# A chain of attention and two MoE layers: dense local attention for the second batch's first 192 rows, sums of squares of weights by TensorE, and rms_g in the split of the normalised x

## The chip, the cores and the metric

One core of one Trainium2 chip runs the whole program. The metric is device time in microseconds of one execution; lower is better. TensorE does the matmuls, VectorE and ScalarE the elementwise steps, GpSimd some products, SyncE (SP) issues every DMA.

## The reference

```python
# attention: q, k, v of (4, 8, 576, 64)
q_d, k_d, v_d = means over 4 rows each            # 144 rows
out_up = repeat(softmax_attention(q_d, k_d, v_d), 4)
scores = scale * q @ k.T, masked to |i - j| < 4
out = out_up + softmax(scores) @ v                # -> x (2304, 512)
# MoE 1: w_in (512, 2048), w_out (2048, 512)
h = x @ w_in; x = (max(h, 0) + alpha * min(h, 0)) @ w_out
# MoE 2: w_gate, w_val (512, 1536), w_out (1536, 512), rms_g (512)
xn = x / sqrt(mean(x * x) + 1e-6) * rms_g
out = (silu(xn @ w_gate) * (xn @ w_val)) @ w_out
```

The kernel takes all inputs as float64 bit patterns (q, k, v as float32) and decodes the weights itself.

## The kernel before, in words

**Tiling.** The 2304 rows are twelve groups of 192 columns, three for each batch; two groups make one of six blocks of 384 columns. `m1` is the first MoE for a block: `h_mm` (L1277) multiplies x by a 128-wide slice of w_in (tile hps), applies the leaky step and splits the result in two fp16 halves (g, ghl), `o_mm` (L1294) multiplies those by w_out (tile acc). `m2` (L1363) is the second MoE: gate and value projections (gps), silu, and the output projection (oacc). Every fp32 operand is split by `split` (L374) into a high and a low fp16 half, one step on ScalarE (L375) and one on VectorE (L376), and a product takes three fp16 matmuls.

**Attention.** Batch 0 goes by the dense path (`Dense`, L702): 96-row windows of scores on TensorE (lsps), exponentials on ScalarE (L889), normalisation, transposes (ltps) and values (lops) on TensorE. Its head tiles T lie in u6 to u9. Groups 3 to 11 go by `local_tasks` (L460): q times seven shifted k on VectorE and GpSimd (L476, six products, alternating), reductions on VectorE (L487), softmax, six products with v (L524), adds on VectorE (L537), transposes on TensorE (L558). The mean-pooled part of batch b is `down(b)`. Group 3, the first 192-column group of batch 1, is staged in the upper slices of wi, since `raw` is not free yet; it is called `l3` and runs beside `down(1)`, ahead of m1.

**Weights.** A `Piece` (L1006) loads a third of a slice in two halves (wr), decodes them (L1048, L1051 on ScalarE, L1053 to L1057 on VectorE) into wc or wo and squares them on ScalarE with an accumulated sum (L1067, tile sqs). The sums over partitions (L349, allps) give a power of two as scale, and the split writes the fp16 halves. w_in has six pieces, w_out six, w_gate, w_val and the second w_out four each. The scale of w_out needs all its squares, so acc matmuls begin after the last. The twelve pieces of the second MoE go through a ring of slots u0 to u12 (`RING`). For gate and value pieces the split multiplies by rms_g as well, one 384-wide quarter at a time (L1188); `rms_tasks` (L1202) normalises x and splits xn (L1259).

**Order.** `m1_first` (L1334) runs the first three h passes of 192 columns (slots h0, h1, h2), then two o passes (o0, o1); the fourth half is `m1(1, CW, CW)` (slot c3). `feed` (L1570) says in which slot background tasks are written. The order in which each engine issues is then set by `issue_order` (L24), a list scheduler with costs per instruction over the whole program; it keeps data dependencies and buffer reuse and reorders everything else. All DMAs stand in SP's one queue. PSUM tiles of tag `at` have two banks.

Of the kernel before, what the change touches and what calls it, by code (L numbers as in the profile page):

```python
# [255 lines left out]
def kernel(  # L256
# [152 lines left out]

    def load_q(g, tag=None):  # L410
        b, t0 = g // CPB, (g % CPB) * T
        t = rawtile([128, 2, T, D], tag, "cq")
        src = bass.AP(tensor=q.tensor, offset=q.offset + b * H * HS + t0 * D,
                      ap=[[TT * D, NC], [2 * HS, HP], [HS, 2], [1, T * D]])
        nc.sync.dma_start(out=t, in_=src)
        return t

    def load_kv(x, g, tag=None):
        b, t0 = g // CPB, (g % CPB) * T
        R = T + 2 * W  # L420
        t = rawtile([128, 2, R, D], tag, "ckv")
        base = x.offset + b * H * HS + (t0 - W) * D

        def part(c0, nc_, h0=0, nh=HP, j0=0, nj=2, nr=R):
            p = HP * c0 + h0
            nc.sync.dma_start(
                out=t[p:p + (nc_ - 1) * HP + nh, j0:j0 + nj, 0:nr],
                in_=bass.AP(tensor=x.tensor, offset=base + c0 * TT * D + (2 * h0 + j0) * HS,
                            ap=[[TT * D, nc_], [2 * HS, nh], [HS, nj], [1, nr * D]]))

        assert b > 0
        if b == B - 1 and t0 + T == TT:
# [27 lines left out]
    def local_tasks(g, engs, tags=(None, None, None), av_pool=True, o_at=None):  # L460
        b, t0 = g // CPB, (g % CPB) * T
# [35 lines left out]
        def sm1():  # L497
            s = st["s"]
            if t0 == 0:
# [3 lines left out]
            if t0 + T == TT:  # L503
# [49 lines left out]
        def trans(half):  # L553
            def f():
# [7 lines left out]
                od = outd_t[b].rearrange("p h (c n) -> p h c n", n=TT // 2)  # L562
                s0 = t0 + half * TH
                for r in range(2):
                    a = s0
                    while a < s0 + TH:
                        o = (r * TT + a) // 4
                        e = a
                        while e < s0 + TH and (r * TT + e) // 4 == o:
                            e += 1  # L570
# [131 lines left out]
    class Dense:  # L702
        def __init__(self, b, place, sd, tsp, smp, lat):
            self.b, self.place, self.sd, self.tsp, self.smp, self.lat = b, place, sd, tsp, smp, lat
            self.st = [{} for _ in range(HP)]

# [143 lines left out]
        def local(self, c, h0, banks):  # L850
# [3 lines left out]
            def s1():  # L854
# [23 lines left out]
                if c:  # L878
                    ls["r"] = raw_p.tile([128, 2 * ns + 2 * CW], F32, tag="raw", name="dls")
                for n, h in enumerate(hs):  # L880
                    tag = ("ob", "xs", "ra", "rb")[h]
                    if c:
# [10 lines left out]
            def s2():  # L893
# [3 lines left out]
                for n, s in enumerate(ls["s"]):  # L897
                    if c:
# [19 lines left out]
            def s4():  # L918
                for n, h in enumerate(hs):
# [8 lines left out]
                    if c:  # L928
# [13 lines left out]
            return [s1, s2, s3, s4]  # L942

# [46 lines left out]
    s1 = const.tile([128, 2 * NF], F32, name="s1")  # L990
    ebw = const.tile([128, NF], F32, name="ebw")
    swi = const.tile([128, NF], F32, name="swi")
    swo = const.tile([128, NF], F32, name="swo")
    s2 = const.tile([128, 3 * NF2], F32, name="s2")
# [8 lines left out]

    sqs = const.tile([128, DM], mybir.dt.bfloat16, name="sqs")

    class Piece:  # L1006
# [53 lines left out]
        def square(self, acc):  # L1060
            for i in range(acc.shape[1]):
                if self.f0 is None:
                    src = self.cv()[:, :, i * 128:(i + 1) * 128]
                    o = sqs.rearrange("p (k c) -> p k c", k=KK)
                else:
                    src, o = self.c[:, i * DM:(i + 1) * DM], sqs
                nc.scalar.activation(out=o, in_=src, func=AF.Square, accum_out=acc[:, i:i + 1])  # L1067
# [3 lines left out]
    RING = (3, 4, 6, 7, 5, 12, 0, 1, 2, 8, 9, 10, 11)  # L1071
# [13 lines left out]
    def prep(p, acc, nsq):  # L1085
# [25 lines left out]
    def scale_out():  # L1111
        x = col(SS + M_WO)
        nc.vector.tensor_reduce(out=x, in_=over_parts(s1[:, NF:2 * NF]), axis=AX.X, op=ALU.add)
# [9 lines left out]
    def split_in(f):  # L1123
# [4 lines left out]
        split(w[:, 0], w[:, 1], c, swi[:, f:f + 1])  # L1128
# [4 lines left out]
    def split_out(f):  # L1133
# [3 lines left out]
        split(w[:, 0], w[:, 1], c, swo[:, f:f + 1])  # L1137
# [7 lines left out]
    gsc = const.tile([128, 8, KK], F32, name="gsc")  # L1145
# [3 lines left out]
    def scale_rg():  # L1149
        nc.vector.tensor_reduce(out=rg2[:, 0:1], in_=rg, axis=AX.X, op=ALU.max, apply_absolute_value=True)  # L1150
        max_parts(rg2[:, 1:2], rg2[:, 0:1])
        nc.vector.tensor_tensor(out=rg2[:, 1:2], in0=rg2[:, 1:2], in1=rg2[:, 1:2], op=ALU.mult)

    def scale2(i):
        def f():
            x = s2[:, 3 * i:3 * i + 3]
            y = s2[:, 3 * i:3 * i + 1]
            nc.vector.tensor_reduce(out=y, in_=over_parts(x), axis=AX.X, op=ALU.max if i < 8 else ALU.add)
            nc.vector.tensor_scalar(out=y, in0=y, scalar1=rg2[:, 1:2] if i < 8 else 1.0, scalar2=LEAST, op0=ALU.mult,
                                    op1=ALU.max)  # L1160
            e, sc_ = eb2[:, i:i + 1], sw2[:, i:i + 1]
            pow2(y, e, sc_, P_W)
            if i < 8:
                nc.vector.tensor_scalar(out=gsc[:, i], in0=rg, scalar1=sc_, scalar2=None, op0=ALU.mult)
                if i < 4:
                    nc.vector.tensor_scalar(out=tsc[:, i:i + 1], in0=e, scalar1=0.5 * 2.0 ** -(P_N + P_W),
                                            scalar2=None, op0=ALU.mult)
            else:
# [3 lines left out]
                nc.vector.tensor_scalar(out=p, in0=p, scalar1=C_INV2, scalar2=None, op0=ALU.mult)  # L1172
# [7 lines left out]
    def split2(i):  # L1180
        def f():
# [3 lines left out]
            if i < 8:  # L1185
# [3 lines left out]
            else:  # L1189
                split(w[:, 0], w[:, 1], p.c, sw2[:, i:i + 1])  # L1190
        return f

    def prep2_tasks():
        out = [[scale_rg]]
        for i in W2_ORDER:
            out.append(prep(p2[i], s2[:, 3 * i:3 * i + 3], 3) + [scale2(i), split2(i)])
# [5 lines left out]
    def rms_tasks(m):  # L1202
# [50 lines left out]
        def xn(e):  # L1253
            def f():
# [4 lines left out]
                split(xh_t[m][:, 0, e], xh_t[m][:, 1, e], x, 2.0 ** P_N)  # L1259
# [103 lines left out]
    def m2(m, slot):  # L1363
# [88 lines left out]
        for tt in range(NT):  # L1452
# [12 lines left out]
            while done < TQ:  # L1465
                b, t = divmod(t_abs + done, TT)
                step = min(TQ - done, TT - t)
                if b == 0:
                    dst = out[b * S + t * NC:b * S + (t + step) * NC, :]
                else:  # L1470
                    dst = bass.AP(tensor=out.tensor, offset=out.offset + (b * S + t) * DM,
                                  ap=[[DM, step], [TT * DM, NC], [1, DM]])
# [36 lines left out]
    def prep_out():  # L1509
        def so(f):  # L1510
# [3 lines left out]
                for t in prep(p, s1[:, NF + 3 * i:min(2 * NF, NF + 3 * i + 3)], min(3, NF - 3 * i))] + [scale_out] + [  # L1514
                    so(f) for f in range(NF)]

    def prep_in(i):
        return prep(p1[i], s1[:, 3 * i:min(NF, 3 * i + 3)], 3 if i < 5 else 1)

    def lane(c):  # L1520
# [3 lines left out]
    pi = [t for p in pi[:3] for t in p] + [lambda: scale_in(0, 9)] + [t for p in pi[3:] for t in p] + [  # L1524
        lambda: scale_in(9, NF)]
# [19 lines left out]
    for h in range(HP):  # L1545
# [5 lines left out]
    wl = wi[:, 8:NF].rearrange("p f a c -> p (f a c)").bitcast(F32)  # L1551
    NQ, NK = 2 * T * D, 2 * (T + 2 * W) * D
    l3 = local(3, tags=(wl[:, 0:NQ], wl[:, NQ:NQ + NK], wl[:, NQ + NK:NQ + 2 * NK]),
               o_at=lambda: p1[5].c[:, KK * 128:KK * 128 + NQ].rearrange("p (t j d) -> p t j d", t=T, j=2))
# [7 lines left out]
    run_all(weave(l3[:-2], d1))  # L1562
    run_all(l3[-2:])
    c1, c2 = lane(1), lane(2)

    def cut(l, at):
# [6 lines left out]
        "h2": po[2] + pr2[0],  # L1573
# [63 lines left out]
```

## Time and profile before

| | before |
|---|---|
| median of 3 runs | 1012.79 us (1012.25 to 1017.23) |
| profiled execution, its own time | 1012.32 us |
| its span | 1010.6 us |
| TensorE, VectorE, ScalarE, GpSimd busy | 930.8, 702.7, 506.8, 147.8 us |

The profiled execution is one run; its span leaves out 1.7 us around the program. PE is TensorE's matmuls, PEld its weight loads, DVE VectorE, ACT ScalarE, POOL GpSimd. A busy TensorE is not TensorE at its peak, as matmuls are pipelined.

### The profile page before, as it was taken

To read this page: it belongs to the slowest core of one execution; us is meant where nothing else is said; L and a number is where in the kernel's file an instruction comes from. 1 tells how busy PE (TensorE), PEld (TensorE's weight loads), DVE (VectorE), ACT (ScalarE), POOL (GpSimd) and SP (SyncE) were. 2 spreads that over 40 slices of the span, in tenths; PEclk is the share of its full clock that TensorE was granted. 3 is DMA by queue.
4 is the path that set the end of the run, shared out by engine and by line. 5 is a ranking of instruction groups with operands and counts; after the bars stand their busy time and mean duration, and the time that the engine had idled before them with its cause. 6 is when DMAs were issued, how large, how long until landed. Compare 5 with 4: busy or idle time off the path is not lost.

```text
span 1010.6 us, 16163 instructions
## 1 busy us (share of the span) xinstructions
PE 930.8 (92%) x6188; PEld 594.4 (59%) x6188; DVE 702.7 (70%) x1482; ACT 506.8 (50%) x1214; POOL 147.8 (15%) x118
## 2 busy tenths in 40 slices
PE   3776777899999999999999999999999999999998
PEld 2554666669976565555656565555556666555454
DVE  3589798999899978999776899983243353442333
ACT  5987879989986473123367232221132432321322
POOL 3522121211001003432100332310000000000000
PEclk9999887899999999999999999999999999999999
DMA  9865228535330143122023111110010000000000
GB/s 257 230 178 186 84 83 276 174 112 157 126 126 13 55 128 104 32 75 67 28 66 96 47 33 47 32 32 1 1 31 1 1 1 1 1 1 4 29 1 31
DMA packets 49821, 74.52 MB, mean 74 GB/s; under 512 B 17532, under 2 KB 30736, under 8 KB 49744
## 3 DMA queue, kind: packets, MB, share of 16 engines
q1 hardware_dynamic: 49744, 73.50, 24.0%
q8 instruction: 48, 0.79, 0.3%
q14 instruction: 29, 0.24, 0.1%
HBM read 68.76 MB, written 4.72 MB: 73 GB/s over the span
## 4 chain that ended last, share of the span: by engine, by line
PE 71%; ACT 11%; DVE 8%; DMA 6%; issue 3%; SPq 1%; POOL 1%; ACTq 0%; POOLq 0%; DVEq 0%
PE gps L1376 22%; PE acc L1297 17%; PE hps L1284 14%; PE oacc L1405 11%; DMA out_dram<-ob 3%; ACT sqs L1067 1%; ACT wr L1048 1%; DVE prod L537 1%; ACT wr L1051 1%; DMA sdv<-in_v_dram 1%; PE lsps L869 1%; SPq L723 1%; ACT dls L889 1%; DMA wr<-in_moe_w_out_dram 1%; PE avps L680 1%
## 5 line engine op out<-in xcount | busy, mean ns | idle before, releaser
L1284 PE MATMUL hps<-xt,wi 128*128 128x192 f16 (+1 forms) x1536 | 336.4, 296 | 9.9 <-DVE g L376 8.2
L1376 PE MATMUL gps<-x,w 128*128 128x384 f16 x1728 | 345.1, 327 | 0.1
L1297 PE MATMUL acc<-ghl,wo 128*128 128x384 f16 (+1 forms) x960 | 251.1, 311 | 4.0 <-ACT ob L1461 2.2
L1376 PEld LDWEIGHTS <-w 128*128 128x128 f16 x1728 | 169.8, 99 | 114.5 <-issue 3.0
L1405 PE MATMUL oacc<-w,uhl 128*128 128x512 f16 x630 | 194.4, 379 | 2.6 <-ACT ob L1461 2.6
L1284 PEld LDWEIGHTS <-wi 128*128 128x128 f16 x1536 | 151.0, 103 | 66.8 <-issue 17.0
L1297 PEld LDWEIGHTS <-wo 128*128 128x128 f16 x1344 | 129.3, 99 | 65.2 <-issue 4.0
L1385 ACT ACTIVATE th<-gps,tsc 128x384 f32<-128x384 f32 x72 | 41.8, 580 | 148.0 <-PE gps L1376 147.8
L1290 DVE SCALAR_TENSOR_TENSOR hps<-g,oma,hps 128x192 f32<-128x192 f32 (+1 forms) x128 | 65.3, 516 | 70.0 <-ACT g L1288 69.5
L1387 DVE SCALAR_TENSOR_TENSOR th<-th,gps 128x384 f32<-128x384 f32 x72 | 39.6, 550 | 94.8 <-ACT th L1385 94.5
L1405 PEld LDWEIGHTS <-uhl 128*128 128x128 f16 x630 | 61.8, 98 | 67.3 <-issue 3.2
L1288 ACT ACTIVATE g<-hps 128x384 f32<-128x384 f32 x96 | 47.0, 489 | 100.4 <-PE hps L1284 100.1
L1396 ACT ACTIVATE uhl<-gps 128x384 f16<-128x384 f32 x72 | 41.7, 579 | 93.5 <-DVE gps L1390 86.4
L476 POOL TENSOR_TENSOR prod<-cq,ckv 128x896 f32<-128x896 f32 x24 | 55.1, 2297 | 211.6 <-DVE ghl L376 56.7
L524 POOL TENSOR_TENSOR prod<-ls,ckv 128x896 f32<-128x896 f32 x24 | 43.7, 1823 | 198.0 <-DVE lo L537 80.3
L1397 DVE TENSOR_TENSOR uhl<-gps,uhl 128x384 f16<-128x384 f32 x72 | 45.3, 629 | 29.0 <-ACT uhl L1396 28.9
L537 DVE TENSOR_TENSOR prod<-prod 128x384 f32<-128x384 f32 (+1 forms) x108 | 62.5, 590 | 3.1 <-POOL prod L524 3.1
L1297 PE MATMUL acc<-g,wo 128*128 128x384 f16 (+1 forms) x384 | 61.9, 286 | 0.7 <-ACT wo L375 0.5
L375 ACT ACTIVATE ghl<-hps,sc 128x384 f16<-128x384 f32 x72 | 41.7, 580 | 37.3 <-DVE hps L1290 36.2
L376 DVE SCALAR_TENSOR_TENSOR ghl<-hps,sc,ghl 128x384 f16<-128x384 f32 x72 | 44.1, 613 | 22.3 <-ACT ghl L375 22.1
L487 DVE TENSOR_REDUCE ls<-prod 128x14 f32<-128x896 f32 x54 | 57.4, 1074 | 0.0
L1048 ACT ACTIVATE wr<-wr 128x768 f32<-128x768 f32 (+1 forms) x48 | 41.8, 876 | 12.2 <-DMA wr<-in_moe_w_in_dram 8.3
(232 smaller groups left out, 1157.8 us busy)
## 6 DMA issues: line engine op xcount, KB each, us to landing
wr<-in_moe_w_out_dram SPq DMA_DIRECT2D x18, 512.0 KB
wr<-in_moe_w_in_dram SPq DMA_DIRECT2D x10, 768.0 KB
wr<-in_moe_w_gate_dram SPq DMA_DIRECT2D x8, 768.0 KB
wr<-in_moe_w_val_dram SPq DMA_DIRECT2D x8, 768.0 KB
ckv<-in_k_dram SPq DMA_DIRECT2D x7, 768.0 KB
ckv<-in_v_dram SPq DMA_DIRECT2D x7, 768.0 KB
wr<-in_moe_w_out_dram SPq DMA_DIRECT2D x20, 256.0 KB
out_dram<-ob SPq DMA_DIRECT2D x13, 256.0 KB
```

Source lines behind the costliest of these rows:

```text
L376: nc.vector.scalar_tensor_tensor(out=lo, in0=src, scalar=s, in1=hi, op0=ALU.mult, op1=ALU.subtract)
L476: engs[i].tensor_tensor(out=pr, in0=view(st["q"][:, j, t:t + TP], [[D, TP], [0, ND], [1, D]]), in1=view(st["k"][:, j, t:t + TP], [[D, TP], ...
L487: nc.vector.tensor_reduce(out=st["s"][:, j, t:t + TP], in_=st.pop(("p", i)), axis=AX.X, op=ALU.add)
L537: add = lambda o, a, c: nc.vector.tensor_tensor(out=o, in0=a, in1=c, op=ALU.add)
L1048: nc.scalar.activation(out=hi.bitcast(F32), in_=hi.bitcast(F32), func=AF.Prelu, scale=2.0 ** -112, alpha=2.0 ** 32)
L1284: nc.tensor.matmul(ps[:, j], wi[:, f + j, a, kk * 128:(kk + 1) * 128], x[:, b_, kk, c0:c0 + n], start=(i == 0), stop=(i == 3 * KK - 1))
L1288: nc.scalar.activation(out=g, in_=ps, func=AF.Relu, scale=-1.0)
L1290: nc.vector.scalar_tensor_tensor(out=ps[:, j], in0=g[:, j], scalar=oma[:, f + j:f + j + 1], in1=ps[:, j], op0=ALU.mult, op1=ALU.add)
L1297: nc.tensor.matmul(acc[e], wo_f(f)[:, a, e * 128:(e + 1) * 128], hl[:, b_], start=(f == 0 and i == 0), stop=(f == NF - 1 and i == 2))
L1376: nc.tensor.matmul(ps, w2_t[i0 + f // 3].rearrange("p a (k c) -> p a k c", k=KK)[:, a, kk, (f % 3) * 128:(f % 3 + 1) * 128], xh[:, b_, kk] ...
L1397: nc.vector.tensor_tensor(out=t1, in0=vp, in1=t0, op=ALU.subtract)
L1405: nc.tensor.matmul(acc[tt], t[:, a, tt * 128:(tt + 1) * 128], w[:, b_, f % 3], start=(f in first and i == 0), stop=(f in last and i == 2))
```

## The change

Three parts. (1) Batch 1's first 192 rows go by the dense path: a new class `DenseHead` replaces `l3`; the tasks stand in slot h2. Groups 4 and 5 then cover the other 384 rows of batch 1 as 32 chunks of 12 rows; loads, masks, pooled adds and stores follow that layout. The dense heads share two tiles in u6 and u7, take q and k through a `prod` tile and probabilities through `raw`; `RING` has another order. (2) `Piece.square` multiplies the upper halves of the fp32 words, read as bf16, by themselves on TensorE, 128 columns at a time (12 matmuls for a full piece, 4 for the last piece of w_in and of w_out), and sums the diagonal on VectorE; there is one scale for a piece instead of one for 128 columns. (3) rms_g, divided by a power of two, moves from the split of the gate and value weights to the split of xn; those pieces are split in one step.

```diff
+    def place_of(g):
+        b, i = divmod(g, CPB)
+        return (b, CW, TT - T, (i - 1) * T) if b == 1 else (b, 0, TT, i * T)
...
-        b, t0 = g // CPB, (g % CPB) * T
+        b, r0, TL, t0 = place_of(g)
...
+    class DenseHead(Dense):
...
+        def alloc(self, h):
+            st, n = self.st[h], 2 * (CW + 2 * W)
+            if "T" in st:
+                return
+            if h % 2 == 0:
+                self.pair = wts.tile([128, UW], F32, tag=f"u{6 + h // 2}", name="T1")
...
+        def load(self, h):
+            self.alloc(h)
+            t = prod_p.tile([QT, 2 * QC + 1, 2, D], F32, tag="prod", name="qk1")
+            self.st[h]["raw"] = t
+            for x, src in enumerate((q, k)):
+                at = src.offset + (self.b * H + 2 * h) * HS
+                for i in range(QC + x):
+                    n = QT if i < QC else W
+                    nc.sync.dma_start(out=t[0:n, x * QC + i], in_=bass.AP(
+                        tensor=src.tensor, offset=at + i * QT * D, ap=[[D, n], [HS, 2], [1, D]]))
+            self.vwin(h, 0)
...
+            for i in range(2 * QC + 1):
+                n = QT if i < 2 * QC else W
+                nc.tensor.transpose(ps[:, i * QT:i * QT + n], t[0:n, i].rearrange("p j d -> p (j d)"), ident[0:n, 0:n])
+            nc.scalar.activation(out=T_[:, 0, W:W + CW], in_=ps[:, 0:CW], func=AF.Copy, scale=scale)
+            nc.scalar.activation(out=T_[:, 1, W:], in_=ps[:, CW:], func=AF.Copy)
...
+            out = [f(g, h) for h0 in (0, 2) for g in (self.load, self.tr) for h in (h0, h0 + 1)]
+            out += [f(od, h) for h in range(HP)]
+            return out + weave(self.local(0, 0, ("a0", "a1")), self.local(0, 2, ("a2", "a3")))
...
         def square(self, acc):
-            for i in range(acc.shape[1]):
...
-                nc.scalar.activation(out=o, in_=src, func=AF.Square, accum_out=acc[:, i:i + 1])
+            ps = ps_t.tile([128, 128], F32, tag="at", name="sqps")
+            nb = self.nf * DM // 128 if self.f0 is not None else KK * self.n // 128
+            up = self.c.bitcast(BF)[:, 1::2]
+            for i in range(nb):
+                x = up[:, i * 128:(i + 1) * 128]
+                nc.tensor.matmul(ps, x, x, start=(i == 0), stop=(i == nb - 1))
+            nc.vector.scalar_tensor_tensor(out=ps, in0=ps, scalar=1.0, in1=ident, op0=ALU.mult, op1=ALU.mult,
+                                           accum_out=acc)
...
-    RING = (3, 4, 6, 7, 5, 12, 0, 1, 2, 8, 9, 10, 11)
+    RING = (3, 4, 5, 6, 7, 12, 0, 1, 2, 8, 9, 10, 11)
...
-            if i < 8:
-                for kk in range(KK):
-                    o = slice(kk * UC, (kk + 1) * UC)
-                    split(w[:, 0, o], w[:, 1, o], p.c[:, o], gsc[:, i, kk:kk + 1])
-            else:
-                split(w[:, 0], w[:, 1], p.c, sw2[:, i:i + 1])
+            split(w[:, 0], w[:, 1], p.c, sw2[:, i:i + 1])
...
-                split(xh_t[m][:, 0, e], xh_t[m][:, 1, e], x, 2.0 ** P_N)
+                split(xh_t[m][:, 0, e], xh_t[m][:, 1, e], x, rgx[:, e:e + 1])
...
-    run_all(weave(l3[:-2], d1))
-    run_all(l3[-2:])
-    c1, c2 = lane(1), lane(2)
+    run_all(d1)
+    c1, c2, c3 = lane(1), lane(2), DenseHead(1).tasks()
...
-        "h2": po[2] + pr2[0],
+        "h2": weave(c3, po[2] + pr2[0]),
```

## Rows read from the trace of the kernel before

**Rows 1.** page, part 1: busy us, share of the span, instructions
```profile
PE 930.8 (92%) x6188; PEld 594.4 (59%) x6188; DVE 702.7 (70%) x1482; ACT 506.8 (50%) x1214; POOL 147.8 (15%) x118
```

**Rows 2.** busy us (instructions) of each engine in stretches, clock, DMA
```profile
60.00:190.00 130.00, 89.82 (x743) 72.96 (x741) 114.60 (x245) 112.22 (x326) 28.04 (x17) 0.88 0.47 151
142.00:190.00 48.00, 34.73 (x302) 30.19 (x302) 42.84 (x97) 45.22 (x120) 9.65 (x7) 0.78 0.60 202
190.00:285.00 95.00, 93.53 (x940) 80.20 (x939) 88.14 (x210) 86.79 (x169) 11.49 (x6) 1.00 0.46 146
285.00:370.00 85.00, 83.90 (x545) 50.53 (x543) 80.31 (x199) 54.06 (x127) 5.64 (x3) 1.00 0.20 66
370.00:460.00 90.00, 86.34 (x519) 49.27 (x518) 80.11 (x145) 28.52 (x73) 29.64 (x14) 1.00 0.27 87
```

**Rows 3.** chain of waits, 98 to 192 us, shares by line
```profile
by line: PE hps L1284 15.5%; issue 11.5%; ACT sqs L1067 7.6%; ACT wr L1051 7.4%; DMA wr<-in_moe_w_gate_dram 6.4%; ACT wr L1048 6.3%; ACT dls L889 4.4%; ACT g L1288 4.1%; ACT g L375 3.7%; ACT xt L375 2.7%; ACT wi L375 2.6%; PE lops L925 2.6%
```

**Rows 4.** groups by line and shape, 60:190; last row: page, part 5
```profile
L476 POOL TENSOR_TENSOR prod<-wi 128x896 f32<-128x896 f32 x3 | 6.6, 2191 | 14.3 <-DVE dsum L656 7.3 <-PE avps L841 5.7 <-PE avps L680 1.3
L524 POOL TENSOR_TENSOR prod<-ls,wi 128x896 f32<-128x896 f32 x3 | 6.7, 2225 | 25.1 <-DVE dsum L655 14.9 <-ACT dd L649 10.2
L476 DVE TENSOR_TENSOR prod<-wi 128x896 f32<-128x896 f32 x3 | 3.3, 1085 | 0.0
L487 DVE TENSOR_REDUCE ls<-prod 128x14 f32<-128x896 f32 x11 | 11.7, 1074 | 0.0
...
L537 DVE TENSOR_TENSOR prod<-prod 128x384 f32<-128x384 f32 (+1 forms) x108 | 62.5, 590 | 3.1 <-POOL prod L524 3.1
```

**Rows 5.** timeline of VectorE near 81 us: start, length, engine, line
```profile
81.38 2.06 DVE L895 TENSOR_SCALAR dlsum<-dlsum 96x8 f32<-96x8 f32 x1
```

**Rows 6.** timelines of VectorE and ScalarE near 136 us
```profile
135.84 1.08 DVE L524 TENSOR_TENSOR prod<-ls,wi 128x896 f32<-128x896 f32 x1
...
137.56 0.71 ACT L375 ACTIVATE wi<-wc,swi 128x512 f16<-128x512 f32 x1
```

**Rows 7.** timeline of TensorE, runs of matmuls; last row: page, part 5
```profile
132.09 0.54 PE L913 MATMUL ltps<-ident,dls 96*102 96x96 f32 x4
132.74 0.95 PE L869 MATMUL lsps<-T 64*96 64x102 f32 x16
134.26 0.62 PE L925 MATMUL lops<-laT,vw 102*64 102x96 f32 x8 [0.57 <-ACT laT L915]
...
163.86 2.14 PE L1284 MATMUL hps<-xt,wi 128*128 128x192 f16 x24 [0.83 <-DVE g L376]
...
L1376 PEld LDWEIGHTS <-w 128*128 128x128 f16 x1728 | 169.8, 99 | 114.5 <-issue 3.0
```

**Rows 8.** group by line and shape, whole span: exponentials
```profile
L889 ACT ACTIVATE dls<-lsps,dlm 96x102 f32<-96x102 f32 x48 | 16.0, 351 | 0.7 <-DVE dlm L875 0.7
```

**Rows 9.** source line L742, SP: ns min/median/max, first and last start
```profile
L742 SPq DMA_DIRECT2D vw<-in_v_dram x50: 265/340/1617, 29.4 to 113.6; - x50
```

**Rows 10.** source line L1376, m2's projections: duration, first and last start
```profile
L1376 PE MATMUL gps<-x,w x1728: 322/326/528, 285.3 to 1000.0; 128*128 128x384 f16 x192
```

**Rows 11.** busy time of source line L1067 (squares) in stretches
```profile
142.00:190.00 48.00, 15.21 (x42) 0.78 0.60 202
190.00:285.00 95.00, 17.37 (x48) 1.00 0.46 146
```

**Rows 12.** groups by line and shape, whole span
```profile
L1290 DVE SCALAR_TENSOR_TENSOR hps<-g,oma,hps 128x192 f32<-128x192 f32 x64 | 25.7, 413 | 5.2 <-ACT g L1288 5.1
L376 DVE SCALAR_TENSOR_TENSOR w<-wc,gsc,w 128x384 f16<-128x384 f32 x32 | 22.1, 706 | 0.5 <-ACT w L375 0.5
L376 DVE SCALAR_TENSOR_TENSOR w<-wc,sw,w 128x1536 f16<-128x1536 f32 x4 | 7.2, 1809 | 1.3 <-ACT w L375 1.3
```

**Rows 13.** waits: who waited for whom, us in total, times, longest
```profile
PE allps L349 <- ACT sqs L1067: 5.0, 2, 4.5
```

**Rows 14.** source line L1297, acc matmuls of the first two m1 passes
```profile
L1297 PE MATMUL acc<-g,wo x384: 242/284/337, 189.0 to 264.1; 128*128 128x384 f16 x96, 128*128 128x192 f16 x96
```

More of the change, by code (lines that the diff above doesn't have):

```diff
@@ L566, in f @@
                     while a < s0 + TH:
-                        o = (r * TT + a) // 4
+                        o = (r * TL + a) // 4
                         e = a
-                        while e < s0 + TH and (r * TT + e) // 4 == o:
+                        while e < s0 + TH and (r * TL + e) // 4 == o:
                             e += 1
@@ L942, in local, with __init__, tr, tasks @@
             return [s1, s2, s3, s4]
+    class DenseHead(Dense):
+        def __init__(self, b):
+            self.b = b
+            self.st = [{} for _ in range(HP)]
+            self.pair = {}
+        def alloc(self, h):
[4 more added lines that the diff above has]
+                self.pair = wts.tile([128, UW], F32, tag=f"u{6 + h // 2}", name="T1")
+            o = h % 2 * (n + QC * 2 * D)
+            st["T"] = self.pair[:, o:o + n].rearrange("p (x s) -> p x s", x=2)
+            st["vw"] = self.pair[0:KW, o + n:o + n + QC * 2 * D].rearrange("p (w j d) -> p w j d", w=QC, j=2)
+            nc.gpsimd.memset(st["T"][:, 1, 0:W], 0.0)
+        def load(self, h):
[9 more added lines that the diff above has]
+            self.vwin(h, 0)
+        def tr(self, h):
+            t, T_ = self.st[h].pop("raw"), self.st[h]["T"]
+            ps = ps_t.tile([128, 2 * CW + W], F32, tag="at", name="tps1")
+            for i in range(2 * QC + 1):
[3 more added lines that the diff above has]
+            nc.scalar.activation(out=T_[:, 1, W:], in_=ps[:, CW:], func=AF.Copy)
+        def tasks(self):
+            def od(h):
+                self.st[h]["od"] = outd_t[self.b][:, h]
+            def f(g, h):
+                return lambda: g(h)
+            out = [f(g, h) for h0 in (0, 2) for g in (self.load, self.tr) for h in (h0, h0 + 1)]
+            out += [f(od, h) for h in range(HP)]
+            return out + weave(self.local(0, 0, ("a0", "a1")), self.local(0, 2, ("a2", "a3")))
     def place():
@@ L1083, with prep @@
     p2 = [w2_piece(i) for i in range(12)]
-    def prep(p, acc, nsq):
+    def prep(p, acc):
         def ld(h):
@@ L1127, in split_in @@
         w = wi[:, f].rearrange("p a (k c) -> p a k c", k=KK)
-        split(w[:, 0], w[:, 1], c, swi[:, f:f + 1])
+        split(w[:, 0], w[:, 1], c, swi[:, f // 3:f // 3 + 1])
     def wo_f(f):
@@ L1136, in split_out @@
         c = p.c[:, (f - p.f0) * DM:(f - p.f0 + 1) * DM]
-        split(w[:, 0], w[:, 1], c, swo[:, f:f + 1])
+        split(w[:, 0], w[:, 1], c, swo[:, f // 3:f // 3 + 1])
     rg2 = const.tile([128, KK], F32, name="rg2")
@@ L1195, in prep2_tasks @@
         for i in W2_ORDER:
-            out.append(prep(p2[i], s2[:, 3 * i:3 * i + 3], 3) + [scale2(i), split2(i)])
+            out.append(prep(p2[i], s2[:, i:i + 1]) + [scale2(i), split2(i)])
         out[-1].append(scale2_all)
@@ L1467, in m2 @@
                 step = min(TQ - done, TT - t)
-                if b == 0:
+                if b == 0 or b == 1 and t < T:
                     dst = out[b * S + t * NC:b * S + (t + step) * NC, :]
                 else:
-                    dst = bass.AP(tensor=out.tensor, offset=out.offset + (b * S + t) * DM,
-                                  ap=[[DM, step], [TT * DM, NC], [1, DM]])
+                    r0, TL = (CW - T, TT - T) if b == 1 else (0, TT)
+                    dst = bass.AP(tensor=out.tensor, offset=out.offset + (b * S + r0 + t) * DM,
+                                  ap=[[DM, step], [TL * DM, NC], [1, DM]])
                 nc.sync.dma_start(out=dst, in_=o[done * NC:(done + step) * NC])
@@ L1523 @@
     pi = [prep_in(i) for i in range(6)]
-    pi = [t for p in pi[:3] for t in p] + [lambda: scale_in(0, 9)] + [t for p in pi[3:] for t in p] + [
-        lambda: scale_in(9, NF)]
+    pi = [t for p in pi[:3] for t in p] + [lambda: scale_in(0, 3)] + [t for p in pi[3:] for t in p] + [
+        lambda: scale_in(3, NP)]
     b0.load(0)
```

92 lines of the change are left out of this document (43 added, 49 removed).

## The prediction

> **What bounds it now.** I read the busy shares first [rows 1]: TensorE works 92% of the span, so at most 80 us of idle time are to be had. The stretches say where they lie [rows 2]: from 190 to 285 us TensorE is busy 93.53 of 95 us, from 285 to 370 us 83.90 of 85, and from 370 to 460 us 86.34 of 90; from 60 to 190 us it is busy 89.82 of 130 us, the last 48 of them at a granted clock of 0.78. In that same stretch VectorE is busy 114.60 us and ScalarE 112.22 us: two engines share the bound there. The chain of waits from 98 to 192 us [rows 3] goes through hps matmuls for 15.5%, but through ScalarE's sqs, wr and g steps for much more. So there are two regimes: before 190 us a microsecond taken off ScalarE and VectorE together brings TensorE's work forward; after 190 us only TensorE's own work counts, and each microsecond of matmul added there costs one.
>
> **Part 1, local attention of group 3 leaves VectorE and GpSimd.** It issues six products of q and k and six of the weights and v, half on each engine, six reductions and eighteen adds, all in the 60 to 190 us stretch. VectorE: six products at 1.085 us, six reductions at 1.074 us, and the two large adds of a unit, 62.5 us over nine groups, so 6.9 us for one [rows 4]: 6.5 + 6.4 + 6.9 = 20 us, its small steps not counted. GpSimd gives up 6.6 + 6.7 = 13.3 us [rows 4]. A GpSimd product also holds VectorE up: a step of eight elements (L895), which is nothing to compute, took 2.06 us at 81.38 us [rows 5], about the length of a GpSimd product. There is a second gain. The group's v is staged in the upper slices of wi, so the last splits of w_in wait for its last product: that product starts at 135.84 us, the last split on ScalarE at 137.56 us [rows 6], and hps pairs for the first window can't end before it. That wait goes; next late is the first window's own xt and the second window's exponentials on ScalarE.
>
> **Part 2, the same rows by the dense path.** It comes back as two head pairs in the h2 slot. They can start when batch 0's T tiles u6 and u7 are free, that is after the scores of its third window; they are needed by the hps matmuls of the second half of block 1, late in the 190 to 285 us stretch. TensorE per pair at full clock [rows 7]: 16 scores 0.95 us, eight transposes twice 0.54, eight values twice 0.62, so 3.3 us, 6.5 for both; twenty input transposes at the same rate (0.54 us for four with the pipe, some 0.085 each after the first) 1.7 us; the six transposes of the old path go. Together about 8 us; at least 6.5, and at most double if they run singly with waits between. ScalarE: 16 exponentials of 0.35 us [rows 8], as many accumulator reads, and 16 copies and splits, by my estimate 15 us; it is busy 86.79 of 95 us after 190 us [rows 2], but part 3 takes 17.4 away from there. VectorE gets some 6 us of reductions, adds and splits, GpSimd four normalisations in front of group 4's products, which wait in its queue. SP: three loads go, 36 come (20 of q and k, 16 of v windows) at 0.34 us an issue [rows 9], some 12 us of SP's queue in a stretch where it mostly waits; behind them stand the raw loads of the second MoE's weights. DMA share there is 0.46 [rows 2], so I cost the transfers at nothing; with that cover gone they would delay the second weights by those 12 us. The ring order makes the first piece of the last matrix wait for T1 in u6: it is needed only in m2, whose first matmul is at 285.3 us [rows 10], and that hides a delay of some 10 us.
>
> **Part 3, sums of squares on TensorE.** ScalarE loses 15.21 us between 142 and 190 us and 17.37 between 190 and 285 us [rows 11], with more before and after. TensorE gains 272 matmuls of 128 columns, each with its own weight load: 64 for w_in, where TensorE is idle, 64 for w_out, mostly before 190 us, and 144 for the second weights, of which I put 120 after 190 us. No such matmul is in the trace. One of 192 columns takes 82 ns (24 in 2.14 us, the last of them 0.25 long, so 1.89 / 23), which is 80 ns of columns at 2.4 GHz and 2 more, so by columns 128 would take 55 ns [rows 7]. From below 55, from above 154 if the load (99 ns each [rows 7]) is not hidden. I take 58, a little over the columns, since the loads are hidden in the row nearest to it. So 120 x 0.058 = 7 us on the path. The Trainium skill (TensorE: Matmul & The Clock Gate, Back-to-back issue gap) gives about 81 ns for a sustained pair of load and 128-column matmul, and no row here has that size; by it these are 9.7 us and the sum below ends 2.7 us later. VectorE gains 24 products with the identity from PSUM, at 0.41 us or less (that is 192 columns [rows 12]): about 0.4 x 24 = 9 us, 3 of them before 190 us. A wait is added: TensorE's queue is in order, so twelve squares of a piece wait for its decode, and hps and acc matmuls stand behind them; and each holds one of the two banks of tag at until VectorE has read it. I cost that at nothing, because the sum over partitions already stood at the same place and waited for sqs in two cases, 5.0 us in all [rows 13].
>
> **Part 4, rms_g in xn.** The eight gate and value pieces are split in one step instead of four: VectorE 32 x 0.706 = 22.1 us against 8 x 1.81 = 14.5 [rows 12], ScalarE alike. This falls after 190 us and pays for most of part 3's VectorE work there. The split of xn takes a column for its scale in 24 steps each on two engines: a tenth of a microsecond each at most, hidden beside m2 matmuls.
>
> **The sum.** From 60 to 190 us ScalarE keeps 112.2 - 15.2 = 97.0 us, VectorE 114.6 - 20 + 3 = 97.6 us. At the shares they have now (0.86 and 0.88) the stretch takes 113 and 111 us: 17 to 19 us less. With the squares before 142 us, the blocking by GpSimd and the small steps I take 22. Lower end 7 (the sqs steps alone are 7.6% of the 94 us chain [rows 3]), upper end 35. After 190 us: +8 and +7, and of the 4.8 us that TensorE idles between 285 and 460 us about 1 comes back as VectorE is ahead. -22 + 15 - 1 = -8 us. The profiled execution took 1012.32 us (span 1010.6), half a microsecond under the median of 1012.79: I predict **1004.5 us**.
>
> **Rivals.** *A, TensorE takes all of it back.* If the first regime shortens by only 15 us, since the chain there also runs through attention's short steps, +15 is paid in full: 1012. For it: the issue share of 11.5% in that chain [rows 3], which less work doesn't shorten; against it: two engines above 85% busy. *B, slower: TensorE waits for decodes.* Ten pieces after 190 us, each with a place where TensorE's queue stands until ScalarE and VectorE have decoded it. The longest such wait now is 4.5 us [rows 13]; at 1.8 us each it is 18 us, so 1004.5 + 18 = 1022. It decides from 1.3 us a piece ((8 + 5) / 10). Against it: ScalarE is freer than before. *C, much faster.* The first window's hps end some 15 us sooner, because nothing of group 3 is in their way, w_out is ready 30 to 35 us sooner, and TensorE is full from 155 us on: -35 + 15 = -20, so 992.5. For it [rows 4, 6]; against it: w_out's raw buffers and down(1) in the same staging, which keep their order. *D, the change doesn't bring its matmuls where I think.* The instruction order is planned anew for the whole program, so stretches that the diff doesn't touch can move by some microseconds either way; that widens each case and is no case of its own.
>
> **How the numbers follow.** Forecast 0.42 (its own range 998 to 1010), A 0.25, B 0.14, C 0.19. Differences under 0.5% (5 us) can't be told from none here. Faster by more: C's 0.19 and most of the forecast, 0.34: 0.53. Slower: B's 0.14 and a little of A: 0.16. The rest is 0.31. The range runs from just under C to between A and B, 990 to 1018; left out are B's upper part and the tail of C.
>
> **What would show it.** The first acc matmul, now at 189.0 us [rows 14], comes near 167 us; sqs is gone from ScalarE; squares follow each other at 55 to 82 ns; TensorE's busy share from there to 285 us stays at 98% or more. It is wrong if the squares stand over 100 ns apart, if TensorE idles before them by over a microsecond a piece, or if the first acc matmul comes less than 15 us earlier.

## The result and the profile after

| | before | after |
|---|---|---|
| median | 1012.52 us (4 runs, 1007.61 to 1017.23) | 986.19 us (4 runs, 985.35 to 988.06) |
| ratio, 95% interval | 1 | 0.974 [0.970, 0.978] |
| span of the profiled execution | 1010.6 us | 983.8 us |

The change wins 26 us, more than the range allowed. The busy shares after (page, part 1, as [rows 1]):

```profile
PE 934.7 (95%) x6562; PEld 605.3 (62%) x6562; DVE 680.0 (69%) x1461; ACT 469.5 (48%) x1099; POOL 139.3 (14%) x120
```

TensorE's busy time hardly moved (930.8 before); its idle time fell by 31 us. The stretches of [rows 2] after, with 60 to 166 us, that is up to the first acc matmul, and 98 to 142 us as two more (length, then busy us and instructions of TensorE, its weight loads, VectorE, ScalarE and GpSimd, then granted clock and DMA):

```profile
60.00:190.00 130.00, 114.52 (x1156) 93.46 (x1156) 112.98 (x288) 122.41 (x345) 16.76 (x18) 0.91 0.59 177
60.00:166.00 106.00, 90.94 (x960) 76.88 (x960) 90.02 (x242) 100.54 (x304) 10.05 (x14) 0.89 0.60 173
98.00:142.00 44.00, 38.16 (x443) 32.08 (x441) 33.49 (x85) 43.67 (x126) 3.65 (x8) 0.96 0.55 156
142.00:190.00 48.00, 46.66 (x462) 36.23 (x462) 43.98 (x104) 44.31 (x105) 8.85 (x6) 1.00 0.58 188
190.00:285.00 95.00, 94.82 (x973) 81.25 (x972) 87.99 (x193) 63.56 (x99) 16.43 (x7) 1.00 0.45 147
285.00:370.00 85.00, 83.94 (x564) 50.00 (x563) 75.83 (x184) 46.72 (x123) 12.33 (x6) 1.00 0.24 72
```

TensorE did 114.5 us in the stretch where it did 89.8, and in its last 48 us the granted clock is 1.00 instead of 0.78: the higher of its two levels, 2.4 GHz, throughout. From 98 to 142 us ScalarE is now the engine without room: 43.67 of 44 us, where it had 35.29 before. For comparison the kernel before up to its own first acc matmul (same view, 60 to 189 us):

```profile
60.00:189.00 129.00, 88.82 (x736) 72.28 (x734) 113.60 (x242) 111.60 (x325) 28.04 (x17) 0.88 0.47 151
```

So that stretch went from 129 to 106 us, VectorE's work from 113.6 to 90.0, ScalarE's from 111.6 to 100.5. ScalarE's share rose from 0.865 to 0.95. The timelines of ScalarE, VectorE and TensorE after show the hand-overs, and two source lines the small step of [rows 5] and the squares:

```profile
106.10 0.75 ACT L375 ACTIVATE wi<-wc,swi 128x512 f16<-128x512 f32 x1
...
151.15 0.73 ACT L375 ACTIVATE wo<-wo,swo 128x512 f16<-128x512 f32 x1
...
165.32 0.35 DVE L941 TENSOR_TENSOR dls<-lops,outd 128x192 f32<-128x192 f32 x1
...
165.88 0.32 PE L1349 MATMUL acc<-g,wo 128*128 128x384 f16 x1
...
L902 DVE TENSOR_SCALAR dlsum<-dlsum x7: 159/168/169, 61.7 to 167.8; 96x8 f32<-96x8 f32 x7
...
65.38 1.30 PE L1121 MATMUL sqps<-wc 128*128 128x128 bf16 x19
...
L1121 PE MATMUL sqps<-wc x212: 217/219/308, 60.2 to 310.8; 128*128 128x128 bf16 x106
```

The last split of w_in on ScalarE starts at 106.1 us (137.56 in [rows 6]). The first split of w_out starts at 151.15; before, that row reads

```profile
187.91 0.71 ACT L375 ACTIVATE wo<-wo,swo 128x512 f16<-128x512 f32 x1
```

37 us sooner, therefore. But the first acc matmul comes only at 165.88 (189.0 in [rows 14]), right behind the first of the four additions L941 (165.3 to 175.2 us) that read the dense path's products out of PSUM: its scores and products use the banks a0 to a3, the same as acc. VectorE's small step takes 169 ns at most; before, one of the five between 60 and 190 us took 2.06 us, at a median of 0.16. The squares stand (1.30 - 0.22) / 18 = 60 ns apart in this run of 19, and last at 310.8 us.

### The profile page after: what moved, and what is told of

It is laid out like the page before. It is cut to its first block, busy times and chain, and to the rows that moved or that the text cites. A ratio compares the mean times of both kernels' runs of the same rounds, so it can differ in the third digit from the quotient of the medians.

```text
span 983.8 us, 16822 instructions
## 1 busy us (share of the span) xinstructions
PE 934.7 (95%) x6562; PEld 605.3 (62%) x6562; DVE 680.0 (69%) x1461; ACT 469.5 (48%) x1099; POOL 139.3 (14%) x120
## 4 chain that ended last, share of the span: by engine, by line
PE 72%; ACT 11%; DVE 8%; DMA 6%; issue 2%; SPq 1%; ACTq 0%; DVEq 0%
PE gps L1428 25%; PE acc L1349 16%; PE hps L1336 13%; PE oacc L1457 12%; DMA out_dram<-ob 3%; DMA sdv<-in_v_dram 2%; ACT dls L896 2%; ACT wr L1103 1%; DVE prod L541 1%; DVE w L376 1%; ACT wr L1106 1%; ACT wi L375 1%; ACT g L1340 1%; PE lsps L876 1%; PE avps L684 1%
## 5 line engine op out<-in xcount | busy, mean ns | idle before, releaser
L1349 PE MATMUL acc<-ghl,wo 128*128 128x384 f16 (+1 forms) x960 | 256.1, 310 | 2.4 <-ACT ghl L375 1.8
L1457 PE MATMUL oacc<-w,uhl 128*128 128x512 f16 x630 | 190.6, 379 | 1.6 <-ACT ob L1513 1.6
L1336 PEld LDWEIGHTS <-wi 128*128 128x128 f16 x1536 | 148.1, 100 | 58.5 <-issue 8.6
L1439 DVE SCALAR_TENSOR_TENSOR th<-th,gps 128x384 f32<-128x384 f32 x72 | 39.7, 551 | 90.5 <-ACT th L1437 89.8
L1349 PE MATMUL acc<-g,wo 128*128 128x384 f16 (+1 forms) x384 | 59.1, 286 | 0.0
L541 DVE TENSOR_TENSOR prod<-prod 128x384 f32<-128x384 f32 (+1 forms) x96 | 50.1, 535 | 2.9 <-POOL prod L528 2.9
L1103 ACT ACTIVATE wr<-wr 128x768 f32<-128x768 f32 (+1 forms) x48 | 42.3, 882 | 20.4 <-DMA wr<-in_moe_w_in_dram 10.4
L491 DVE TENSOR_REDUCE ls<-prod 128x14 f32<-128x896 f32 x48 | 51.1, 1075 | 0.0
```

The lines of the kernel that those rows point to most:

```text
L491: nc.vector.tensor_reduce(out=st["s"][:, j, t:t + TP], in_=st.pop(("p", i)), axis=AX.X, op=ALU.add)
L541: add = lambda o, a, c: nc.vector.tensor_tensor(out=o, in0=a, in1=c, op=ALU.add)
L1103: nc.scalar.activation(out=hi.bitcast(F32), in_=hi.bitcast(F32), func=AF.Prelu, scale=2.0 ** -112, alpha=2.0 ** 32)
L1336: nc.tensor.matmul(ps[:, j], wi[:, f + j, a, kk * 128:(kk + 1) * 128], x[:, b_, kk, c0:c0 + n], start=(i == 0), stop=(i == 3 * KK - 1))
L1349: nc.tensor.matmul(acc[e], wo_f(f)[:, a, e * 128:(e + 1) * 128], hl[:, b_], start=(f == 0 and i == 0), stop=(f == NF - 1 and i == 2))
L1457: nc.tensor.matmul(acc[tt], t[:, a, tt * 128:(tt + 1) * 128], w[:, b_, f % 3], start=(f in first and i == 0), stop=(f in last and i == 2))
```

## The experiments

Each was timed beside the kernel before, whose medians there lay between 1010.75 and 1015.65 us.

| | median us | ratio to before, 95% interval |
|---|---|---|
| changed kernel | 986.19 | 0.974 [0.970, 0.978] |
| e1 dense path alone; another order | 1010.72; 1004.47 | 0.999 [0.996, 1.003]; 0.987 [0.982, 0.992] |
| e2 squares alone | 1005.80 | 0.993 [0.991, 0.996] |
| e3 rms_g alone | 1007.17 | 0.993 [0.991, 0.996] |
| e4 squares and rms_g | 997.28 | 0.985 [0.981, 0.990] |
| f3 dense path and squares | 993.11 | 0.980 [0.974, 0.987] |
| e9 dense path and rms_g | 1006.94 | 0.994 [0.991, 0.998] |
| before, two other orders | 1013.32, 1006.89 | 1.001 [0.999, 1.004], 0.998 [0.995, 1.001] |
| changed, three other orders | 994.23, 996.57, 989.74 | 0.985 [0.982, 0.987], 0.988 [0.984, 0.991], 0.977 [0.971, 0.982] |
| f1 without group 3; another order | 983.40; 984.15 | 0.971 [0.965, 0.976]; 0.969 [0.965, 0.972] |
| f2 dense path in hps' banks | 1013.56 | 1.001 [0.998, 1.004] |
| e5 later squares four times | 1029.26 | 1.017 [1.012, 1.022] |
| e6 w_in's squares seven times | 1004.03 | 0.992 [0.990, 0.995] |
| e7 more matmuls in the dense path | 1023.47 | 1.010 [1.007, 1.013] |

**One part at a time.** The theory was "idle": the dense path now stands ahead of the first acc matmul, where TensorE has idle time, and costs nothing; the rival was the prediction's "paid".

```diff
 # e1: hunks of part 1 alone; squares and rms_g as before
-    run_all(weave(l3[:-2], d1))
+    run_all(d1)
 # e2: hunks of part 2 alone; the two sums meet in scale2
+            nc.vector.tensor_scalar(out=y, in0=over_parts(y), scalar1=rg2[:, 1:2] if i < 8 else 1.0, scalar2=LEAST,
+                                    op0=ALU.mult, op1=ALU.max)
 # e3: hunks of part 3 alone
+            nc.vector.tensor_scalar(out=y, in0=y, scalar1=1.0, scalar2=LEAST, op0=ALU.mult, op1=ALU.max)
 # e4: changed kernel, hunks of part 1 undone
-    run_all(d1)
+    run_all(weave(l3[:-2], d1))
```

> The kernel before with the dense path for group 3 alone; sums of squares stay on ScalarE, rms_g stays in the weights. Both engines that bound the first stretch were needed for the 23 us by which the first acc matmul came earlier, so with VectorE and GpSimd alone relieved it moves by 8 to 14 us, from 189 to about 178. Theory 'idle' (the dense path runs where TensorE idles before the first acc matmul and costs nothing there): the end moves by as much as the first acc matmul or a little more, to about 1001 us. Rival 'paid' (as predicted, 8 us of dense path on TensorE's full stretch): the end moves by 8 us less than the first acc matmul, to about 1009 us, and dense matmuls lie behind the first acc matmul.

> The kernel before with the sums of squares on TensorE alone; group 3 stays on VectorE and GpSimd, rms_g in the weights. ScalarE alone relieved: first acc matmul 5 to 12 us earlier, about 180. Both theories take the squares behind the first acc matmul as paid, about 130 matmuls of 57 ns, 7.4 us: the end comes to about 1010 us. If squares cost nothing there either (rival 'all of it is hidden'), the end moves with the first acc matmul, to about 1003 us.

> The kernel before with rms_g in the split of the normalised x alone. It takes about 7.6 us off VectorE and as much off ScalarE behind the first acc matmul, where TensorE sets the pace. Theory: no change beyond 2 us, 1011 to 1013; first acc matmul where it was (189). Rival (VectorE's earliness shortens TensorE's idle time later, 17.5 us of it between 369 and 588 us): up to 4 us faster, 1008.

> The changed kernel with group 3 back on VectorE and GpSimd (squares on TensorE and rms_g in the split of x stay). Theory 'idle': the dense path brought most of the 26 us and cost nothing, so this is about as e2: 1007 to 1010, first acc matmul 5 to 12 us earlier than 189. Rival 'paid': the dense path gave back 8 us, so without it the loss is 8 us smaller than the shift of the first acc matmul: if that comes to 180, the end comes to 1000 or below.

Only e4 came out where a theory had it ("paid": 1000 or below). The times of e1 and e3 lie near "paid" and near e3's rival, but not by their mechanisms. e1 brought the first acc matmul to 170.7 us, 18 us sooner, and won nothing that can be told: m2's first pass took 99.7 us (266 to 366) where it takes 83.7 before (285 to 369). TensorE idles 14.8 us of it, against 1.1 before; the second row is before:

```profile
266.00:366.00 100.00, 85.24 (x521) 50.97 (x519) 95.31 (x215) 60.16 (x140) 15.92 (x7) 0.91 0.25 78
285.00:369.00 84.00, 82.90 (x539) 49.97 (x537) 79.31 (x197) 53.72 (x126) 5.64 (x3) 1.00 0.20 66
```

TensorE's longest waits in e1's pass (who waited for whom, us, times, longest) name what came late:

```profile
PE allps L349 <- ACT sqs L1123: 9.5, 2, 7.3
PE gps L1432 <- DVE th L1443: 2.0, 2, 1.2
```

With sqs still on ScalarE the second weights are late, and TensorE's queue stands in front of their sum over partitions for 9.5 of the 16 us; in the changed kernel that wait is 0.2 us. e2 won 7 us and e4 15. e3 is the odd one: rms_g touches nothing ahead of the first acc matmul but a few steps on 128x4 or smaller, and yet that matmul came at 180.9 instead of 189.0. (From 369 to 588 us TensorE idles 5.2 us in the kernel before, not the 17.5 of e3's expectation.)

**The order.** So next the work was left alone and only the plan changed: one constant of the scheduler, the wait it assumes between two VectorE instructions.

```diff
-             ("DVE", "DVE"): 127,
+             ("DVE", "DVE"): 124,     # o_before_124, o_after_124; 130 and 120 in the others
```

> The kernel before with the same instructions, planned anew: one constant of the planner, the wait it assumes between two VectorE instructions, is 124 ns instead of 127. With rms_g alone the first acc matmul came 8 us earlier although nothing that this part touches runs before it, so theory 'plan' says that the order alone moves the time: this comes out 3 to 10 us away from 1012, in the first stretch, with TensorE's total work unchanged. Theory 'work' (each part earns what it takes off the engines, and rms_g's 5 us came from the freed VectorE and ScalarE) expects 1012 within 2 us.

> The kernel before, the same constant at 130 ns. As the last: 'plan' expects 3 to 10 us away from 1012 and another value than at 124, 'work' expects 1012 within 2 us.

> The changed kernel with the same constant at 124 ns. 'plan': a spread of several us about 986, on the slow side above all if 986 is a lucky order. 'work': 986 within 2 us.

> The changed kernel with the constant at 130 ns. As the last. If the three orders of the changed kernel lie on average 15 to 20 us under the three of before, that is what the work is worth, and the rest of the 26 us is the order.

> The changed kernel planned with 120 ns in place of 127: a fourth order of the same instructions. If 986 is a lucky order, 991 to 998; if the other two were unlucky, 984 to 990.

The changed kernel's four orders lie at 986.2, 989.7, 994.2 and 996.6, mean 991.7; the intervals of the best two don't meet that of the worst, and the order as written is the lowest. Those of before lie at 1012.5, 1013.3 and 1006.9, mean 1010.9, with intervals that meet. The work is worth 1010.9 - 991.7 = 19 us, with a few us of scatter; the rest of the 26 is the order. e3's 8 us in the first acc matmul are of the size of the changed kernel's spread there (165.9 to 173.0), so a single part's few microseconds can't be read off a single order.

**Where added TensorE time is paid.** Some 22 to 24 us of matmuls of 128 columns were added in one of three places at a time.

```diff
 # e5, e6: in square(); R = 4 for the second weights (e5), 7 for w_in (e6), 1 for the others
-            for i in range(nb):
+            for i in [i for _ in range(R) for i in range(nb)]:
 # e7: in DenseHead.tr, ahead of the transposes; ps is overwritten by them
+            up = t.rearrange("p i j d -> p (i j d)").bitcast(BF)[:, 1::2]
+            for i in [i for _ in range(27) for i in range(2 * QC)]:
+                x = up[:, i * 128:(i + 1) * 128]
+                nc.tensor.matmul(ps[:, 0:128], x, x, start=True, stop=True)
```

> The changed kernel with the squares of the second weights issued four times over (the sum of the last pass is the one used): 432 more matmuls of 128 columns, 24 us at the 56 ns measured, nearly all behind the first acc matmul. Theory 'late is paid, early is free': 24 us slower than the three orders of the changed kernel (986 to 997), so 1010 to 1021. Rival 'TensorE has room everywhere' (the squares behind the first acc matmul lay in idle time too): under 10 us slower, 990 to 1003.

> The changed kernel with the squares of w_in alone issued seven times over: 384 more matmuls, 22 us at full clock and 41 us at the lower clock that TensorE had there, all ahead of the hps matmuls. 'late is paid, early is free': under 10 us slower than 986 to 997, what it costs is the latency ahead of the splits of w_in. Rival (added TensorE time is paid wherever it stands): 22 us slower, 1008 to 1019.

> The changed kernel with 432 further matmuls of 128 columns and 96 rows (24 us at 56 ns) in group 3's dense path, ahead of the transposes of its q and k; their results are overwritten. Theory 'idle' (the dense path runs where TensorE idles before the first acc matmul, so its own 8 us cost nothing there): under 8 us slower than 986 to 997. Rival 'paid' (as predicted): 24 us slower, 1010 to 1021.

Against the mean of the changed kernel's orders e5 costs 37.6 us, e6 12.3, e7 31.8. Late squares are paid and more; the time in front of w_in is half paid; and "idle" falls for the dense path, whose added matmuls are paid in full and more although they stand ahead of the first acc matmul. e7's timeline of TensorE shows them back to back, (7.38 - 0.22) / 125 = 57 ns apart, and the first acc matmul at 206.6 us, behind them. Ahead of that point TensorE idled 38.5 us, against 37.1 in the mean of the changed kernel's four orders, so the added matmuls found no idle time (the execution profiled is the slowest of its ten, 1027.7 us):

```profile
184.82 7.38 PE L986 MATMUL tps<-qk 96*128 96x128 bf16 x126
...
206.61 0.32 PE L1353 MATMUL acc<-g,wo 128*128 128x384 f16 x1
```

In e5 the waits between 171 and 301 us are those of the prediction's rival B, in a small size:

```profile
PE allps L349 <- DVE sqps L1122: 5.6, 5, 2.6
PE acc L1349 <- ACT x L1363: 2.8, 3, 1.4
```

**The price of the dense path, and the pairs.** The bank row at 165 us suggested a theory "gate": the dense path ends last because it holds acc's banks.

```diff
 # f1 (f1_order_124 with 124 as above)
-    c1, c2, c3 = lane(1), lane(2), DenseHead(1).tasks()
+    c1, c2, c3 = lane(1), lane(2), [lambda: nc.gpsimd.memset(xt(1)[:, :, :, CW:], 0.5)]
 # f2
-            return out + weave(self.local(0, 0, ("a0", "a1")), self.local(0, 2, ("a2", "a3")))
+            return out + weave(self.local(0, 0, ("w", "w")), self.local(0, 2, ("w", "w")))
 # f3: hunks of parts 1 and 2; e9: hunks of parts 1 and 3; e1_order_124: e1 with 124
```

> The changed kernel with group 3's local attention left out altogether: its half of xt is set to a constant, and that half of the windows' outputs is not the reference's. Theory 'gate' (the dense path ends last before the first acc matmul because it holds the PSUM banks of acc): first acc matmul at 152 to 156, where w_out's first split ends, and 8 us or more under the 986 to 997 of the changed kernel's orders, so 975 to 986. Rival 'free' (TensorE is full with hps matmuls meanwhile, so a later acc costs nothing, and the path's own work lies in idle time): first acc matmul earlier but 986 to 997 as now. As predicted (8 us of TensorE): 978 to 989.

> The changed kernel without group 3 (its half of xt a constant, so that half of the outputs is not the reference's), planned with 124 ns. If the dense path costs about the 8 us of TensorE time predicted for it, wherever it stands: 979 to 989, and the mean of both orders 6 to 10 us under the changed kernel's 992. If it is free: 988 to 996.

> The changed kernel with the dense path's scores, transposes and values in the two PSUM banks of hps instead of the four of acc. 'gate': the first acc matmul no longer waits for the path, comes at about 153, and the kernel gains some us: 978 to 990. Rival 'free': acc earlier, time as now or, as hps has to share its banks, 5 to 15 us slower (995 to 1010).

> The changed kernel with rms_g back in the second weights: dense path and squares alone. What rms_g is worth in this company: 7.6 us less on VectorE and ScalarE each behind the first acc matmul. Theory 'work hidden' (predicted): 986 to 997 as the changed kernel's orders. Rival 'the second weights' preparation sets the pace behind the first acc matmul' (the dense path alone and the kernel without squares lost 13 to 20 us of TensorE time there): 5 us or more slower than their mean of 992, with TensorE idle over 10 us between the first acc matmul and the end of m2's first pass.

> The changed kernel with the sums of squares back on ScalarE (dense path and rms_g in the split of x stay). The dense path alone brought the first acc matmul to 170.7 us, but TensorE then idled 26 us of the 100 in m2's first pass, against 6 before, and nothing was won. Theory 'the dense path hands the bound to ScalarE, late with the second weights': the same here, a little milder as rms_g's splits take 7.6 us off ScalarE: first acc matmul near 171, 1000 to 1008 in all. Rival 'that stall was bad luck of the order': 990 to 997, as the changed kernel with 7 us less of squares on TensorE.

> The kernel before with the dense path alone, planned with 124 ns. If the idle time in m2's first pass (26 us, behind two late sums of squares on ScalarE) belongs to this combination: 1005 to 1013 again, with over 12 us lost between the first acc matmul and the end of m2's first pass. If it was the luck of one order: 990 to 1002.

f1's two orders, mean 983.8, price the dense path at 991.7 - 983.8 = 7.9 us. "Gate" is not borne out: without the path the first acc matmul still came at 166.3 and 165.1, since the plan then brought w_out later (first splits at 165.5 and 164.3). f2 freed acc's banks and had the first acc matmul at 164.5, again behind a later w_out (163.7), so whether the banks alone would hold acc up stays open. f2's first pass of m2 took 106.2 us against 85.6, with the same kind of wait as in e1:

```profile
PE allps L349 <- DVE sqps L1122: 6.3, 1, 6.3
PE gps L1428 <- DVE uhl L1449: 2.9, 1, 2.9
```

f3 shows rms_g worth 993.1 - 991.7, nothing in this company. The dense path alone (mean of two 1007.6) is worth 3 us, squares alone 5, both together 1010.9 - 993.1 = 18, more than their sum. e9, without the squares, comes to 1006.9, but loses its time elsewhere than e1: it takes 110.6 us from the first acc matmul to m2, where the changed kernel takes 96.6, and TensorE idles 9.5 us there, mostly for splits of ghl and 0.3 us for sqs. (The 26 and 6 us of idle time that expectations give for e1 and the kernel before in m2's first pass are 14.8 and 1.1 by the rows above; e1's other order, 1004.5, idles 10.4 us there, 5.8 of them for sqs.) Without the dense path much of the gain is there too: e4's squares and rms_g are worth 1010.9 - 997.3 = 13.6, so rms_g makes 8.5 us beside the squares alone and nothing beside both. Apart from the dense path alone these are single orders, and orders of one work lay up to 10 us apart: the sign of such differences can be read, their size hardly. None of the runs that compute the whole result beats the changed kernel.

## Why the prediction was wrong

The sign and the two prices on TensorE were right; the first stretch was mis-sized, and the order was left out. Stage by stage, from the first acc matmul and the first matmuls of m2's first and second pass in each profiled execution (means over orders, us):

| | to first acc | to m2 | m2's first pass | rest | span |
|---|---|---|---|---|---|
| before, 3 orders | 190.1 | 94.9 | 82.1 | 641.4 | 1008.6 |
| changed, 4 orders | 169.4 | 96.6 | 85.1 | 638.7 | 989.8 |
| without group 3, 2 orders | 165.7 | 92.8 | 84.4 | 639.4 | 982.4 |

- **Two regimes: right behind the first acc matmul, half right ahead of it.** Behind it TensorE is busy 94.82 of 95 us. Ahead of it either part alone brings most: first acc matmul at 170.7 and 168.3 us in e1's orders, 175.8 in e2, 173.9 in e4, 169.4 with all parts, so the two gains overlap instead of adding up. In e1 what ScalarE then still owes (its sqs) falls due as TensorE's wait in m2's first pass, and takes most of the gain.
- **Part 2, +8 us: right size, wrong place.** f1 gives 7.5 us in the spans, 7.9 in the medians, half ahead of the first acc matmul and half behind. I had put it wholly between 190 and 285 us; it began at 146 us, and 76 of its 108 matmuls ran ahead of the first acc matmul, with the last addition at 175.2. It shares acc's banks and stands before it in the program; that this is the reason isn't shown. e7 shows that its matmuls cost their length there too.
- **Part 3, +7 us: right.** 132 squares lie behind the first acc matmul of the changed kernel, 132 x 57 ns = 7.5 us. The Trainium skill (TensorE: Matmul & The Clock Gate, Back-to-back issue gap) gives about 81 ns a pair at 128 columns; the measured 57 to 60 ns decide, and by the columns of a neighbouring row the prediction was nearer. The wait added for decodes was costed at nothing, and is 0.2 us in m2's first pass.
- **Part 4: right,** nothing that can be told beside the other two (f3).
- **The failed step: "At the shares they have now (0.86 and 0.88) the stretch takes 113 and 111 us ... I take 22. ... upper end 35."** f1 is the change without the dense path. Its first acc matmul comes 24.4 us sooner, not far from the 22, and in the changed kernel it came at 165.9, near the 167 that I had named. But in f1 472 hps matmuls are done before it instead of 409 (means of the traces): 63 x 82 ns [rows 7] is 5.2 us more of the late work, which the term left out, 29.6 in all. Behind it the program got 1.8 us shorter, where +7.2 for f1's 127 squares and -5.2 for hps make +2.0: 3.8 us, where I had 1 (TensorE's idle time there fell by 2.8). So -22 was really about -30 and -1 really -4; the sum is -30 + 8 + 7 - 4 = -19, as the orders show. The shares were taken as fixed. f1 up to its first acc matmul:

```profile
60.00:166.00 106.00, 86.86 (x925) 74.19 (x924) 89.74 (x234) 96.54 (x280) 14.32 (x11) 0.94 0.57 180
```

ScalarE's work is what I had (96.54, predicted 97.0), but its share is 0.91 and not 0.86; VectorE has 89.74 us left, predicted 97.6. That 22 came near 24.4 all the same is owed to the 3 to 5 us put on top of the 17 to 19 by hand. With the dense path's exponentials ScalarE's work in the changed kernel is 100.5 us, and its share 0.95. That ScalarE gets further is part 1's doing, as the stretch from 98 to 142 us shows, ahead of the dense path's first exponential (154 us in the changed kernel, 159 in e1): before, e1 (dense path alone), f1, and e4 (the other two parts), in this order:

```profile
98.00:142.00 44.00, 33.88 (x309) 27.60 (x308) 38.30 (x80) 35.29 (x101) 9.39 (x5) 0.89 0.27 87
98.00:142.00 44.00, 34.39 (x339) 29.32 (x339) 32.79 (x75) 43.55 (x130) 3.65 (x8) 0.88 0.39 111
98.00:142.00 44.00, 38.46 (x434) 32.13 (x434) 34.62 (x88) 42.71 (x130) 3.37 (x4) 0.96 0.42 133
98.00:142.00 44.00, 32.72 (x267) 26.74 (x267) 41.14 (x82) 31.68 (x84) 7.08 (x4) 0.75 0.31 94
```

With group 3 gone from VectorE and GpSimd, ScalarE works 41.9 to 43.9 of the 44 us in every order of e1, f1 and the changed kernel; with group 3 in place, 35.3 to 36.5 in the three orders of before, and 31.68 in e4. There VectorE ended 8.1 of ScalarE's 12.3 idle us, with these as the longest:

```profile
ACT wi L375 <- DVE prod L524: 2.8, 2, 2.4
ACT g L375 <- DVE hps L1286: 2.5, 2, 2.0
ACT dls L889 <- DVE dlm L875: 2.1, 2, 1.7
```

So group 3's work held ScalarE up. There are signs that ScalarE held VectorE up as well: from 60 to 170 us VectorE works 95.69 us before, 84.39 in e1 and 102.87 in e4, ScalarE 92.79, 106.71 and 91.68 (rows in this order):

```profile
60.00:170.00 110.00, 75.29 (x638) 60.13 (x636) 95.69 (x215) 92.79 (x278) 21.77 (x14) 0.92 0.47 147
60.00:170.00 110.00, 88.85 (x830) 72.91 (x826) 84.39 (x210) 106.71 (x335) 11.31 (x15) 0.95 0.49 140
60.00:170.00 110.00, 84.33 (x772) 68.35 (x770) 102.87 (x252) 91.68 (x262) 22.84 (x14) 0.80 0.53 160
```

This side is weaker, as e3, which relieves neither engine there, has VectorE at 99.98. Either way 0.86 and 0.88 were no limits: ScalarE reaches 0.97 in e1, VectorE 0.94 in e4. Which of VectorE's and GpSimd's steps did it isn't separated by a run: the small step of 2.06 us is gone, and the last w_in split came 31 us sooner, where in e4 w_in splits still wait for group 3's product (first row of the waits).
- **Rival C** had this: w_out ready 30 to 35 us sooner (37 here), 992.5 us; the mean of the orders is 991.7. TensorE was full from 155 us on too, 34.14 of the 35 us up to 190, but part of that time went to the dense path, which C left behind acc.
- **Rival A and B** didn't happen. B's wait is real, though: it shows in e1, e5 and f2.
- **D, "no case of its own", is the other failed step.** The order as written lies 5.5 us under the mean of four: of the 18 us by which the forecast missed, 5.5 are the luck of the order. The range's low end of 990 held that mean, not the order that was timed.

What stays open: why one order is better than another, whether acc's banks held the first acc matmul up, and which of VectorE's and GpSimd's steps held ScalarE up most.

## What to carry to other kernels

Two engines at 86 and 88% needn't be at a limit: one may stay under 100% only because it waits for the other, so don't scale a stretch by today's shares. Take work off both: here 3 and 5 us alone became 18 together. With the first part alone, what the second engine still owed turned up as a wait of TensorE 100 us later. And where a scheduler plans the whole program anew, time several plans of the same work before crediting a part with a few microseconds.

## What the runs showed of the hardware

- A matmul of 128 columns with its own weight load, both operands bf16 taken at a stride of two elements, follows the last in 57 to 60 ns; the stride showed no price in its weight loads (97 ns, where fp16 weights without a stride take 99 [rows 7]).

```profile
L1121 PEld LDWEIGHTS <-wc x212: 96/97/181, 59.9 to 310.6; 128*128 128x128 bf16 x106
```

- An accumulated output of VectorE comes as an instruction of its own: behind each product with the identity (0.29 us) stands a read of the accumulator. Timeline of VectorE after:

```profile
166.24 0.29 DVE L1122 SCALAR_TENSOR_TENSOR sqps<-sqps,ident 128x128 f32<-128x128 f32 x1
166.45 0.14 DVE L1122 DVE_READ_ACCUMULATOR sqps<-sqps,ident 128x1 f32 x1
```

24 of both are about 10 us of VectorE, against the 9 predicted.
